# One PSUM tile per bank, and a new start-up, in a fused attention and channel-mix kernel

## The chip, the cores and the metric

The kernel runs on one core of one Trainium2 chip. The metric is the device time of one execution in microseconds (us). All runs that are compared below are in the fast state, with a granted TensorE clock of 0.96 to 1.00 of full; one run that was not is named where it occurs.

A ratio below is the mean time of one kernel's fast runs over the mean of the fast runs of the kernel before from the same rounds, with a 95% interval. It is therefore not quite the ratio of the medians that stand beside it.

Engine names: PE is TensorE, PEld its weight loads, DVE is VectorE, ACT is ScalarE, POOL is GpSimd, SP is SyncE.

## The reference

```python
# q, k, v: (8 batches, 8 heads, 576, 64) float32
q_s = softmax(q, axis=-1)
k_s = softmax(k, axis=2)                       # over the sequence
kv  = einsum('bhsd,bhse->bhde', k_s, v)
x   = einsum('bhsd,bhde->bhse', q_s, kv)       # then reshaped to (8, 576, 512)
x_prev = x shifted by one row, zero first
xk = mu_k * x + (1 - mu_k) * x_prev
xr = mu_r * x + (1 - mu_r) * x_prev
k   = maximum(xk @ w_k, 0)                     # 512 -> 1024
out = sigmoid(xr @ w_r) * (k * k @ w_v)        # 1024 -> 512
```

## The kernel before

The kernel loads q, k and v per batch in two groups of four heads, does the attention with small matmuls, and mixes rows into xk and xr. The rows then go through the second part in units of 512 (or 256) rows: K matmuls (`xk @ w_k`), relu on ACT, a square on DVE, R matmuls (`xr @ w_r`), tanh on ACT (the sigmoid), V matmuls (`k*k @ w_v`), and a gate on DVE that reads the V result from PSUM. A small planner written in the kernel orders every operation of every engine before it emits them. A framework below it sets the semaphores (counters by which one engine waits for another) from the tiles that each instruction touches.

The results of K, R and V lie in PSUM, the memory that takes the matmuls' results, in four banks that are used in turn. Before, these four banks are two tiles of two banks each; in batch 0 the kv matmuls borrow the same banks as a pair:

```python
banks = [psum.tile([128, 2, 512], F32, name=f"bank_{x}") for x in "abcd"]
ps = {"mm": [banks[2 + i // 2][:, i % 2, :] for i in range(4)],      # K, R, V
      "att": [t[:, :, :] for t in banks[0:2]],
      "early": [t[:, :, :] for t in banks[2:4]]}                     # kv of batch 0
# ... cut ...
def k_part(kf, fc, cts):                       # K: four matmuls of 512 columns
    for ct in cts:
        nc.tensor.matmul(bank(kf)[:, 0:n], lhsT=wk_bf[:, ct, fc * 128:(fc + 1) * 128],
                         rhs=xs[0][:, ct, c0:c0 + n], start=(ct == 0), stop=(ct == CT - 1))
# ... cut ...
nc.scalar.activation(out=rels[rel.index][:, 0:n], in_=bank(kf)[:, 0:n], func=ACT.Relu, ...)
# ... cut ...
nc.vector.scalar_tensor_tensor(out=ots[ot.index][:], in0=ths[th.index][:], scalar=1.0,
                               in1=bank(vps), op0=ALU.add, op1=ALU.mult)
```

The start-up: batch 0 comes in twelve pieces of 288 KB on the queues of SP and ACT, and the weights come on POOL's queue behind a wait on one of those pieces.

```python
gate = [first[GATE]]                           # GATE = 7: the second piece of v, group 0
# ... cut ...
if h == u == 0:
    tc.add_manual_dep(ld.ins, gate[0].made.ins.name, sync)
# in the planner: every operation's key is drawn forward by when its users are due, loads too
if closed:
    for o in after.get(op, ()):
        op.key = min(op.key, o.key - op.lat - HOP - SPARE)
```

The softmax here doesn't subtract the row's maximum and nothing guards it: scores larger than these inputs give would overflow.

## Time and profile before

| | before |
|---|---|
| time, median of 3 runs | 230.28 us (230.2 to 231.39) |
| span of the profiled run | 228.7 us |
| PE busy | 196.1 us, 86% |
| TensorE work, columns at 512 per 0.216 us (worked out) | 181.8 us |
| stalls between matmuls (worked out) | 33.7 us |

The page of the profile gives the busy time of each engine and, in 40 slices of 5.7 us, its busy share in tenths. These are its first lines for the kernel before:

```profile
span 228.7 us, 3591 instructions
...
PE 196.1 (86%) x1281; PEld 98.1 (43%) x1281; DVE 164.9 (72%) x368; ACT 152.3 (67%) x228; POOL 41.6 (18%) x65
...
PE   0076999967899878998979999999999999999881
...
DVE  1774855898899959989787989699578538832521
ACT  2658689798898688587427897957775664452430
...
```

PE is the busiest engine by far, and yet many slices stand at 7 or 8. A 9 stands for 90% or more, so it does not tell whether PE is full in the later slices, where DVE and ACT are half idle; the windows do.

The view of windows sums the busy time in stretches. Its columns are the stretch and, for each engine, busy us with the number of instructions, then the granted clock, the share of the DMA engines and GB/s:

```profile
...
core 0: us, PE busy (x) PEld busy (x) DVE busy (x) ACT busy (x) POOL busy (x), PEclk, DMA share, GB/s
34.00:54.00 20.00, 17.85 (x154) 9.16 (x152) 16.13 (x35) 18.46 (x27) 10.41 (x15) 1.00 1.04 400
54.00:94.00 40.00, 35.17 (x221) 17.02 (x221) 34.87 (x71) 33.86 (x47) 10.11 (x14) 1.00 0.90 317
94.00:214.00 120.00, 115.75 (x728) 56.82 (x727) 89.65 (x193) 74.92 (x114) 3.61 (x5) 1.00 0.32 80
...
```

From 94 us on ACT is busy 75 of 120 us and DVE 90, and PE still loses time. From 34 to 54 us ACT is nearly full.

The view of waits of the kernel before, from 54 us on and for PE, says whom each matmul waited for (total us, times, longest):

```profile
...
engine line waited for: us in total, times, longest us
PE bank_c L617 <- ACT rel_a L602: 1.6, 2, 1.3
PE bank_d L617 <- DVE ot_c L664: 1.2, 1, 1.2
PE bank_c L658 <- ACT th_b L653: 1.2, 2, 1.0
PE bank_c L658 <- DVE ot_b L664: 1.1, 2, 0.8
...
PE bank_c L648 <- ACT rel_c L602: 0.6, 1, 0.6
...
```

The matmuls wait for many different readers of PSUM: relu (`rel`) and tanh (`th`) on ACT, the gate (`ot`) on DVE. This list alone does not say whether the reader used the bank that the matmul wanted. Two readings do. The first is the built program: each semaphore wait names the instruction that must have finished, and 146 of its waits have as their only common ground a PSUM tile of which the two instructions touch different banks. The second is the chain of work that ended last. These are its pieces around 212 us (start, length, what):

```profile
...
210.17 1.74 PE bank_d L658 x8
...
211.99 0.70 DVE ot_c L664
...
212.73 1.04 PE bank_d L658 x4
...
```

Two V matmul groups are in flight here, one in each bank of tile `bank_d`. The first ends, the gate `ot_c` reads its bank, and only then do the last four V matmuls start, though they write the other bank. They wait for nothing else.

The start-up, from the timeline of the kernel before (start, length, engine, line, operation, and in brackets the idle time before it with what ended it):

```profile
...
4.66 2.51 POOL L351 DMA_DIRECT2D wk_bf<-in_moe_w_k_dram  x4
...
17.22 0.67 ACT L406 CAST vv_b<-raw_f 128x576 bf16<-128x576 f32 x1 [1.18 <-DMA raw_f<-in_v_dram]
...
19.38 0.67 ACT L406 CAST vv_b<-raw_f 128x576 bf16<-128x576 f32 x1
...
21.54 1.16 PE L429 MATMUL bank_d<-vv_b,ek_b 64*128 64x129 bf16 x18
...
22.63 1.44 PE L617 MATMUL bank_c<-xk,wk_bf 128*128 128x512 bf16 x4
...
26.49 1.02 PE L617 MATMUL bank_d<-xk,wk_bf 128*128 128x512 bf16 x4
...
34.98 1.03 PE L658 MATMUL bank_c<-wv_bf,k_a 128*128 128x512 bf16 x4
...
```

The weights are issued at 4.66 us, in the middle of batch 0's loads. v of group 1 is cast at 17.22 and 19.38 us when its pieces land, its kv matmuls run at 21.54 us, K runs steadily from 26.49 us, and V starts at 34.98 us.

### The profile page before, as it was taken

How to read it: one execution, taken by the hardware profiler on the slowest of the kernel's cores; microseconds unless marked ns; L12 is line 12 of the kernel's file. 1: busy time of each engine (PE TensorE's matmuls, PEld its weight loads, DVE VectorE, ACT ScalarE, POOL GpSimd, SP SyncE). 2: the span in 40 equal slices, each digit the busy share in tenths (PEclk: the TensorE clock that was granted, in tenths of full speed). 3: DMA queues.
4: the chain of work that ended last, by engine and by line, in shares of the span. 5: the costliest groups of instructions: out<-in, count | busy, mean ns of one | idle time of the engine just before them, and what ended most of it. 6: DMA issues, size and time to landing. Idle time of an engine off the chain costs nothing. (4 is left out here: it accounts for less than half of the span.)

```text
span 228.7 us, 3591 instructions
## 1 busy us (share of the span) xinstructions
PE 196.1 (86%) x1281; PEld 98.1 (43%) x1281; DVE 164.9 (72%) x368; ACT 152.3 (67%) x228; POOL 41.6 (18%) x65
## 2 busy tenths in 40 slices
PE   0076999967899878998979999999999999999881
PEld 0053444533354434543446544444543454444530
DVE  1774855898899959989787989699578538832521
ACT  2658689798898688587427897957775664452430
POOL 8615437344322122112000000000000000000000
PEclk9999999999999999999999999999999999999999
DMA  6999999999999858868372040222042122403404
GB/s 199 299 292 357 209 338 390 402 399 402 393 400 404 290 193 232 237 159 268 109 195 46 4 92 0 64 63 62 0 94 67 25 49 46 92 0 91 94 3 92
DMA packets 16722, 40.88 MB, mean 179 GB/s; under 512 B 2360, under 2 KB 5184, under 8 KB 16704
## 3 DMA queue, kind: packets, MB, share of 16 engines
q0 software_dynamic: 8896, 27.40, 37.3%
q1 hardware_dynamic: 7200, 12.39, 20.1%
q10 hardware_dynamic: 608, 0.85, 1.2%
q8 instruction: 10, 0.16, 0.3%
q14 instruction: 8, 0.07, 0.1%
HBM read 33.82 MB, written 9.44 MB: 189 GB/s over the span
## 5 line engine op out<-in xcount | busy, mean ns | idle before, releaser
L617 PEld LDWEIGHTS <-wk_bf 128*128 128x128 bf16 x320 | 30.6, 98 | 39.0 <-issue 9.9
L617 PE MATMUL bank_d<-xk,wk_bf 128*128 128x512 bf16 (+1 forms) x160 | 37.1, 357 | 3.5 <-DVE ot_c L664 1.2
L617 PE MATMUL bank_c<-xk,wk_bf 128*128 128x512 bf16 (+1 forms) x160 | 37.6, 360 | 2.3 <-ACT rel_a L602 1.6
L658 PEld LDWEIGHTS <-k_a 128*128 128x128 bf16 x144 | 13.5, 97 | 18.9 <-issue 3.0
L658 PE MATMUL bank_c<-wv_bf,k_a 128*128 128x512 bf16 x80 | 20.2, 379 | 1.3 <-ACT th_b L653 1.0
L658 PEld LDWEIGHTS <-k_b 128*128 128x128 bf16 x144 | 13.5, 97 | 17.5 <-issue 3.1
L648 PEld LDWEIGHTS <-xr 128*128 128x128 bf16 x144 | 13.3, 98 | 17.3 <-issue 2.4
L658 PE MATMUL bank_d<-wv_bf,k_b 128*128 128x512 bf16 x80 | 20.2, 379 | 0.3 <-DVE ot_b L664 0.3
L648 PE MATMUL bank_c<-wr_bf,xr 128*128 128x512 bf16 x72 | 18.5, 379 | 0.8 <-ACT rel_c L602 0.6
L648 PE MATMUL bank_d<-wr_bf,xr 128*128 128x512 bf16 x72 | 18.5, 379 | 0.5 <-ACT th_b L653 0.5
L658 PE MATMUL bank_d<-wv_bf,k_a 128*128 128x512 bf16 x64 | 16.1, 379 | 1.6 <-DVE ot_c L664 0.9
L658 PE MATMUL bank_c<-wv_bf,k_b 128*128 128x512 bf16 x64 | 16.2, 379 | 1.2 <-DVE ot_b L664 0.8
L602 ACT ACTIVATE rel_c<-bank_d 128x512 bf16<-128x512 f32 (+1 forms) x17 | 9.3, 547 | 8.7 <-PE bank_d L617 8.1
L602 ACT ACTIVATE rel_b<-bank_c 128x512 bf16<-128x512 f32 (+1 forms) x17 | 9.5, 559 | 5.9 <-PE bank_c L617 5.2
L653 ACT ACTIVATE th_a<-bank_c 128x512 f32<-128x512 f32 x10 | 6.0, 598 | 7.3 <-PE bank_c L648 3.4
L602 ACT ACTIVATE rel_a<-bank_c 128x512 bf16<-128x512 f32 (+1 forms) x14 | 7.5, 539 | 4.0 <-PE bank_c L617 3.8
L653 ACT ACTIVATE th_a<-bank_d 128x512 f32<-128x512 f32 x8 | 4.8, 599 | 6.4 <-PE bank_d L648 5.7
L602 ACT ACTIVATE rel_a<-bank_d 128x512 bf16<-128x512 f32 (+1 forms) x13 | 7.4, 570 | 1.8 <-PE bank_d L617 1.6
L606 DVE TENSOR_TENSOR k_a<-rel_b 128x512 bf16<-128x512 bf16 (+1 forms) x14 | 5.6, 404 | 3.9 <-ACT rel_b L602 3.7
L443 PE MATMUL bank_a<-ident,qs_a 128*128 128x128 bf16 x72 | 5.8, 230 | 2.8 <-DVE qs_a L421 2.8
L447 ACT COPY qt_a<-bank_a 128x1152 bf16<-128x1152 bf16 x5 | 5.6, 1117 | 3.7 <-PE bank_a L443 3.7
L653 ACT ACTIVATE th_b<-bank_c 128x512 f32<-128x512 f32 x8 | 4.8, 598 | 4.8 <-PE bank_c L648 4.5
(208 smaller groups left out, 389.0 us busy)
## 6 DMA issues: line engine op xcount, KB each, us to landing
out_dram<-ot_a SPq DMA_DIRECT2D x24, 128.0 KB, 2.4
out_dram<-ot_b SPq DMA_DIRECT2D x24, 128.0 KB, 2.4
out_dram<-ot_c SPq DMA_DIRECT2D x24, 128.0 KB, 2.4
raw_a<-in_q_dram POOLq DMA_DIRECT2D x3, 576.0 KB, 8.7
raw_b<-in_q_dram POOLq DMA_DIRECT2D x3, 576.0 KB, 7.0
raw_c<-in_k_dram POOLq DMA_DIRECT2D x3, 576.0 KB, 7.7
raw_d<-in_v_dram POOLq DMA_DIRECT2D x3, 576.0 KB, 8.5
raw_e<-in_k_dram POOLq DMA_DIRECT2D x3, 576.0 KB, 9.7
```

The source lines that it names most:

```text
L443: nc.tensor.transpose(out=transposed()[:, j, :], in_=qss[qs.index][:, j, :], identity=ident[:])
L447: nc.scalar.copy(out=qts[qt.index][:], in_=transposed()[:, 0:J, :])
L602: nc.scalar.activation(out=rels[rel.index][:, 0:n], in_=bank(kf)[:, 0:n], func=ACT.Relu, scale=HALF_ROOT)
L606: nc.vector.tensor_tensor(out=k2s[k2.index][:, fc, 0:n], in0=rels[rel.index][:, 0:n], in1=rels[rel.index][:, 0:n], op=ALU.mult)
L617: nc.tensor.matmul(bank(kf)[:, 0:n], lhsT=wk_bf[:, ct, fc * 128:(fc + 1) * 128], rhs=xs[0][:, ct, c0:c0 + n], start=(ct == 0), stop=(ct == ...
L648: nc.tensor.matmul(bank(rps), lhsT=xs[1][:, ct, c:c + 128], rhs=wr_bf[:, ct, :], start=(ct == 0), stop=(ct == CT - 1))
L653: nc.scalar.activation(out=ths[th.index][:], in_=bank(rps), func=ACT.Tanh, scale=0.5)
L658: nc.tensor.matmul(bank(vps), lhsT=k2s[k2.index][:, ft, 128 * m:128 * m + 128], rhs=wv_bf[:, ft, :], start=(ft == 0), stop=(ft == FT - 1))
```

## The change

Its intent: each matmul bank becomes its own tile, so that only accesses to one bank order each other; batch 0's pieces come in a fixed order with batch 0 ahead of the weights; the mask work of mu leaves DVE and ACT's queue for POOL.

```diff
-MU_KEY = (0.5, 1.9, LATE, LATE)
+FILL = 0
# planner
-                if closed:
+                if closed and not op.size:          # loads keep their own key
# PSUM
-    banks = [psum.tile([128, 2, 512], F32, name=f"bank_{x}") for x in "abcd"]
-    ps = {"mm": [banks[2 + i // 2][:, i % 2, :] for i in range(4)],
-          "att": [t[:, :, :] for t in banks[0:2]], "early": [t[:, :, :] for t in banks[2:4]]}
+    ps = {"mm": [psum.tile([128, 512], F32, name=f"mm_{x}") for x in "abcd"],
+          "att": [psum.tile([128, 2, 512], F32, name=f"att_{x}") for x in "ab"]}
+    def kv_of(slot, hf):                            # kv of batch 0: two tiles now
+        if slot.pool == "early":
+            return ps["mm"][2 * slot.index + hf][:]
+        return bank(slot)[:, hf, :]
# masks
-        nc.gpsimd.memset(mu_mask[:]..., 0.0)
+        nc.vector.memset(mu_mask[:]..., 0.0)
-            nc.scalar.dma_start(out=mu_rows[...], in_=ap)
+            nc.gpsimd.dma_start(out=mu_rows[...], in_=ap)
-            nc.vector.tensor_copy(out=mu_mask[...], in_=mu_rows[...])
-            nc.vector.tensor_scalar(out=mu_mask[...], in0=mu_rows[...], ...)
+            nc.gpsimd.tensor_copy(out=mu_mask[...], in_=mu_rows[...])
+            nc.gpsimd.tensor_scalar(out=mu_mask[...], in0=mu_rows[...], ...)
# cut: two reciprocals where kv lies in two tiles, planned durations, an unused filler (FILL = 0)
```

The wait that holds the weights is the same text as before (`GATE = 7`). What changes is when its piece comes: before, the planner drew that half of v to the head of SP's queue; with fixed order it is the eighth piece. That the planner does this is seen in the order of the built programs, not in the diff.

More of the change, by code (lines that the diff above doesn't have):

```diff
@@ L233 @@
     ots = buffers("ot", [128, C], F32)
-    banks = [psum.tile([128, 2, 512], F32, name=f"bank_{x}") for x in "abcd"]
-    ps = {"mm": [banks[2 + i // 2][:, i % 2, :] for i in range(4)],
-          "att": [t[:, :, :] for t in banks[0:2]], "early": [t[:, :, :] for t in banks[2:4]]}
+    ps = {"mm": [psum.tile([128, 512], F32, name=f"mm_{x}") for x in "abcd"],
+          "att": [psum.tile([128, 2, 512], F32, name=f"att_{x}") for x in "ab"]}
     def bank(slot):
-        return ps[slot.pool][slot.index]
+        return ps[slot.pool][slot.index][:]
+    def kv_of(slot, hf):
+        if slot.pool == "early":
+            return ps["mm"][2 * slot.index + hf][:]
+        return bank(slot)[:, hf, :]
     xs = [const.tile([128, CT, RING], BF16, name=n) for n in ("xk", "xr")]
@@ L300, in emit_mask_zeros @@
     def emit_mask_zeros():
-        nc.gpsimd.memset(mu_mask[:].rearrange("p m s c e -> p (m s c e)"), 0.0)
+        nc.vector.memset(mu_mask[:].rearrange("p m s c e -> p (m s c e)"), 0.0)
     def emit_late_consts():
@@ L310 @@
     plan.add("ACT", 2.0, 2.0, 1.5, emit_warm, [zero])
-    mu_load = plan.add("POOL", 1.2, 1.2, -9, emit_mu_load, size=8.0)
-    identity = plan.add("POOL", 0.6, 0.8, -8, emit_identity)
-    consts = plan.add("DVE", 0.5, 0.6, -9, emit_consts, [identity])
+    mu_load = plan.add("POOL", 1.2, 1.2, -9.2, emit_mu_load, size=8.0)
+    identity = plan.add("POOL", 0.6, 0.8, -9.1, emit_identity)
+    consts = plan.add("DVE", 0.2, 0.3, -9, emit_consts, [identity])
     late_consts = plan.add("DVE", 0.6, 0.7, LATE, emit_late_consts)
-    mask_zeros = plan.add("POOL", 2.2, 2.3, -7, emit_mask_zeros)
+    mask_zeros = plan.add("DVE", 1.8, 1.9, 0, emit_mask_zeros)
     mu_slot = Slot("mm")
@@ L328, in emit_mu_rows_load @@
             ap = bass.AP(tensor=src.tensor, offset=src.offset + 256 * u, ap=[[0, 64], [1, 256]])
-            nc.scalar.dma_start(
+            nc.gpsimd.dma_start(
                 out=mu_rows[64 * u:64 * u + 64, m, :, :].rearrange("p c e -> p (c e)"), in_=ap)
@@ L335, in emit_mu_mask, with filler @@
             r = slice(64 * u, 64 * u + 64)
-            nc.vector.tensor_copy(out=mu_mask[r, m, 0, :, r], in_=mu_rows[r, m, :, :])
-            nc.vector.tensor_scalar(out=mu_mask[r, m, 1, :, r], in0=mu_rows[r, m, :, :],
+            nc.gpsimd.tensor_copy(out=mu_mask[r, m, 0, :, r], in_=mu_rows[r, m, :, :])
+            nc.gpsimd.tensor_scalar(out=mu_mask[r, m, 1, :, r], in0=mu_rows[r, m, :, :],
                                     scalar1=-1.0, scalar2=1.0, op0=ALU.mult, op1=ALU.add)
     mu_t = plan.add("PE", 0.2, 0.4, -500, emit_mu, [mu_load, consts], [mu_slot])
-    mu_done = plan.add("DVE", 0.08, 0.17, LATE, emit_mu_copy, [mu_t], gives=[mu_slot])
+    mu_done = plan.add("DVE", 0.08, 0.17, 0, emit_mu_copy, [mu_t], gives=[mu_slot])
     mu_masked = []
     for m in range(2):
-        o = plan.add("ACT", 0.9, 0.9, MU_KEY[m], lambda m=m: emit_mu_rows_load(m), size=131.0)
-        mu_masked.append(plan.add("DVE", 1.0, 1.1, MU_KEY[2 + m], lambda m=m: emit_mu_mask(m),
+        o = plan.add("POOL", 1.4, 1.4, -9.5 + m, lambda m=m: emit_mu_rows_load(m), size=131.0)
+        mu_masked.append(plan.add("POOL", 1.6, 1.7, -2 + m, lambda m=m: emit_mu_mask(m),
                                   [o, mask_zeros]))
+    def filler(slot):
+        for _ in range(2):
+            nc.tensor.matmul(bank(slot)[:, 0:128], lhsT=ident[:], rhs=ident[:], start=True,
+                             stop=True)
+    for _ in range(FILL):
+        slot = Slot("mm")
+        plan.add("PE", 0.11, 0.2, 2 * LATE, lambda slot=slot: filler(slot), [identity], [slot],
+                 [slot])
     def weight_part(dst, src, n, u, c0, c1):
@@ L429, in kv @@
                     nc.tensor.matmul(
-                        bank(kvp)[:, hf, 0:129],
+                        kv_of(kvp, hf)[:, 0:129],
                         lhsT=eks[ek.index][r, j, :, :].rearrange("p u d -> p (u d)"),
@@ L434, in recz @@
         def recz():
-            nc.vector.reciprocal(out=rzs[rz.index][:, :, None],
-                                 in_=bank(kvp)[:, :, 128:129])
+            if kvp.pool == "att":
+                nc.vector.reciprocal(out=rzs[rz.index][:, :, None],
+                                     in_=bank(kvp)[:, :, 128:129])
+            else:
+                for hf in range(2):
+                    nc.vector.reciprocal(out=rzs[rz.index][:, hf:hf + 1],
+                                         in_=kv_of(kvp, hf)[:, 128:129])
         def transposed():
@@ L480, in attention @@
         kvm = plan.add("PE", 0.63, 0.7, pe_key, kv, expk + castv, [kvp], [ek, vv])
-        zdone = plan.add("DVE", 0.066, 0.15, step + 2, recz, [kvm], [rz])
+        zdone = plan.add("DVE", 0.08 * (2 if b == 0 else 1), 0.25 if b == 0 else 0.16, step + 2, recz, [kvm], [rz])
         def weights_of(wp, m, hf, s):
             nc.vector.scalar_tensor_tensor(
-                out=wps[wp.index][:, hf, s, :], in0=bank(kvp)[:, hf, 0:128],
+                out=wps[wp.index][:, hf, s, :], in0=kv_of(kvp, hf)[:, 0:128],
                 scalar=rzs[rz.index][:, hf:hf + 1], in1=mu_mask[:, m, s, 2 * g + hf, :],
@@ L571, in attention @@
                                 [xb] if hf == 0 else [], [xps[hf]]))
-        o = plan.add("DVE", 0.1, 0.19, step + 6, edge, evs)
+        o = plan.add("DVE", 0.11, 0.19, step + 6, edge, evs)
         xdiff = plan.add("DVE", 0.66, 0.755, step + 6, diff, [o], [xd])
```

## The prediction

> **What bounds it now.** TensorE. The page shows PE busy 196.1 of 228.7 us at full granted clock. Counting each matmul at the back-to-back pace of the trace (512 columns per 0.216 us), the program holds 179.4 us of TensorE work (my sum). The rest is about 19 us without work before the first K matmul at 22.6 us (timeline), 23 us of stalls between matmuls afterwards, and a tail of some 4 us. Windows view: from 34 to 54 us ACT is busy 18.5 of 20 us; from 94 to 134 us ACT and DVE have slack (25.9 and 33.7 of 40), yet PE still loses time.
>
> **Main term: PSUM tiles.** Before, one tile holds two banks, and the built program orders accesses by tile: 146 semaphore waits have as their only reason an access to the other bank of the same tile; in the changed program I count none. The Trainium skill, "PSUM — Partial Sum Buffer", "The four PSUM rules", says "Each bank is a separate physical SRAM", so these waits protect nothing; no run has shown that yet. Laid beside the trace, such waits hold back PE's start by 13.8 us in all after 22.6 us: 6.1 at K matmuls (L617), 5.6 at V (L658), 2.1 at R (L648). In the chain, the last V half waits from 222.2 to 223.0 us for a gate on DVE (ot_b) that reads the other bank. 4.3 us lie before 94 us, where ACT or data would often be the next wait (I count half, 2 us), 9.5 us after, where little else stalls PE (85%, 8 us).
>
> **Start-up.** Before, v's second half of group 0 is loaded first (SyncE, 0.74 us), so the weights' gate opens near 4.6 us and wk competes with batch 0; v of group 1 is cast only at 17.2 and 19.4 us, and K matmuls run steadily only from 26.5 us. After, the 12 batch-0 pieces go q, q, k, v, k, v and wk waits for the eighth, near 9 to 10 us. At the pace seen (0.85 us per 288 KB piece) all land by 13 to 14 us; kv of group 1 moves from 21.5 to about 16 us, steady K to about 20. But the weights come no sooner: DMA is nine tenths busy to 75 us, wv landed near 32.8 us before, and V cannot start much before 33. What survives is ACT and DVE work done ahead of the ACT-bound stretch: 2.5 us.
>
> **Small terms.** The mask arithmetic (8 instructions, 2.4 us) leaves DVE, the 1.8 us memset goes to it while idle: little. On GpSimd it is off the chain unless mask r is late. Later loads in fixed order: slots gate them, neutral.
>
> **Sum.** 230.3 - 8 - 2 - 2.5 gives about 217.5 us, 8 in 10 between 212.5 and 223. Chances: faster by over 2% 0.94, within 2% 0.05, slower 0.01.
>
> **What would show it.** Right: PE stalls from 94 us on fall from about 11 us to 2 to 4; PE waits on DVE ot and ACT rel/th nearly vanish from the waits view; wk issue moves from 4.7 to 9 or 10 us; kv of group 1 at 15 to 17 us; first V at 32 to 34 us. Wrong: stalls just move to true waits (same bank's reader), or first V comes after 35 us.
>
> **What would make it wrong.** Late weights stalling the first unit; ACT saturation giving back early gains; mm slots held long by mask r.

## The result and the profile after

| | before | after |
|---|---|---|
| time, median | 230.83 us (230.2 to 231.46, 4 runs) | 213.62 us (213.51 to 214.27, 4 runs) |
| ratio of fast runs | | 0.926 (0.9222 to 0.9299) |
| span of the profiled run | 228.7 us | 211.9 us |
| PE busy | 86% | 90% |

The same lines of the page, for the kernel after:

```profile
span 211.9 us, 3596 instructions
...
PE 190.7 (90%) x1281; PEld 97.1 (46%) x1281; DVE 163.0 (77%) x363; ACT 152.0 (72%) x228; POOL 45.1 (21%) x76
...
PE   0269788978999999999999999999999999999990
...
DVE  4958651999999999999988999698679448942521
ACT  3694796999899999697449987946794665452430
...
```

From the eleventh slice on PE stays at 9, up to the last one.

The windows of the kernel after; the last stretch ends where its matmuls near their end:

```profile
...
54.00:94.00 40.00, 39.92 (x299) 20.09 (x297) 39.29 (x84) 36.31 (x50) 12.24 (x18) 1.00 1.00 375
94.00:197.00 103.00, 103.00 (x659) 51.47 (x657) 80.87 (x175) 69.10 (x106) 2.12 (x3) 1.00 0.30 77
...
```

From 94 us on PE is busy 103.00 of 103 us, against 115.75 of 120 before. In the stretch from 54 to 94 us it is busy 39.92 of 40 us, up from 35.17, with DVE at 39.29 and ACT at 36.31: these two now do more in the same time as well.

The waits of PE over the whole span of the kernel after, part of its eight lines:

```profile
...
PE mm_c L443 <- ACT vv_a L420: 2.0, 1, 2.0
PE mm_c L636 <- DVE xk L579: 2.0, 1, 2.0
PE mm_d L677 <- DMA wv_bf<-in_moe_w_v_dram: 1.3, 1, 1.3
PE mm_c L636 <- ACT rel_a L621: 1.1, 1, 1.1
...
PE mm_c L636 <- ACT rel_c L621: 0.3, 1, 0.3
```

All of these lie before 54 us; the same view from 54 us on has no line at all. Of the reads that PE waited for before, those of DVE's gate and of tanh are gone.

The start-up of the kernel after, from its timeline:

```profile
...
7.86 0.94 POOL L340 COPY mu_mask<-mu_rows 64x256 f32<-64x256 f32 x1 [2.91 <-DMA mu_rows<-in_moe_mu_k_dram]
...
11.64 2.54 POOL L365 DMA_DIRECT2D wk_bf<-in_moe_w_k_dram  x4 [1.62 <-DMA raw_d<-in_v_dram]
...
14.12 1.23 ACT L420 CAST vv_b<-raw_f 128x576 bf16<-128x576 f32 x2
...
19.25 0.60 PE L636 MATMUL mm_c<-xk,wk_bf 128*128 128x512 bf16 x2
...
```

And its first V matmuls, from a later part of the same timeline:

```profile
...
32.36 1.02 PE L677 MATMUL mm_d<-wv_bf,k_a 128*128 128x512 bf16 x4 [1.28 <-DMA wv_bf<-in_moe_w_v_dram]
...
```

The weights are issued at 11.64 us, behind the masks on POOL and the eighth piece. v of group 1 is cast at 14.12 us, its kv matmuls follow at 15.40 us (before 21.54), steady K starts at 19.25 us (before 26.49). But V starts at 32.36 us, only 2.6 us sooner than before, and it waited for wv to land.

A sum that I worked out for several kernels from the start times of the matmuls: the stall before a matmul is the time from the start of the one before it, less that one's columns at 512 per 0.216 us, the pace at which matmuls follow each other in these traces (columns count half for the matmuls that use half of the rows and run in pairs). The prediction names this pace too, but its 179.4 us of work comes from one about 1% faster; at 0.216 us the kernels hold 181.8 us. "Other bank" is the part of it that a wait for the other bank of the same tile brought about, beyond what the true waits would have cost at that place. A second count by a slightly different rule gives 154 waits and 14.5 us for the kernel before, in place of 146 and 13.8, and none for after; the figures are good to about that much. Up to 22 of the 1281 matmul records are missing in the traces of some experiments; their work is counted from the program. The columns "tiles only", "paired tiles" and "early weights" are experiments of the next section.

```
stalls of PE, us            before   tiles only   paired tiles   after   early weights
0 to 54 us                   15.4       15.0          15.1        13.2       11.7
54 to 94 us                   7.0        0.9           4.1         1.6        1.4
94 us to the end             11.3        1.7           9.3         1.6        1.7
all                          33.7       17.6          28.5        16.4       14.7
of it "other bank"           13.8        0             9.3         0          0
```

### The profile page after: what moved, and what is told of

Same layout as the page of the kernel before. It is cut to its first block, busy times and chain, and to the rows that moved or that the text cites. A ratio compares the mean times of both kernels' runs of the same rounds, so it can differ in the third digit from the quotient of the medians.

```text
span 211.9 us, 3596 instructions
## 1 busy us (share of the span) xinstructions
PE 190.7 (90%) x1281; PEld 97.1 (46%) x1281; DVE 163.0 (77%) x363; ACT 152.0 (72%) x228; POOL 45.1 (21%) x76
## 4 chain that ended last, share of the span: by engine, by line
PE 70%; DMA 15%; DVE 6%; ACT 3%; SPq 1%; issue 1%; POOL 1%; DVEq 0%; POOLq 0%
PE mm_b L677 8%; PE mm_a L677 7%; PE mm_a L636 6%; PE mm_c L636 6%; PE mm_b L636 6%; PE mm_d L677 6%; PE mm_c L677 5%; PE mm_d L636 5%; PE mm_d L667 5%; DMA raw_l<-in_v_dram 4%; DMA wr_bf<-in_moe_w_r_dram 4%; DMA raw_d<-in_v_dram 4%; DMA wk_bf<-in_moe_w_k_dram 3%; PE mm_c L667 3%; PE mm_a L667 3%; PE att_b L443 2%
## 5 line engine op out<-in xcount | busy, mean ns | idle before, releaser
L636 PE MATMUL mm_c<-xk,wk_bf 128*128 128x512 bf16 (+1 forms) x88 | 21.7, 359 | 3.4 <-DVE xk L579 2.0
L677 PEld LDWEIGHTS <-k_a 128*128 128x128 bf16 x144 | 13.3, 98 | 16.3 <-issue 1.6
L636 PE MATMUL mm_a<-xk,wk_bf 128*128 128x512 bf16 (+1 forms) x84 | 20.5, 359 | 0.1
L667 PEld LDWEIGHTS <-xr 128*128 128x128 bf16 x144 | 13.3, 98 | 15.3
L636 PE MATMUL mm_d<-xk,wk_bf 128*128 128x512 bf16 (+1 forms) x72 | 18.0, 361 | 0.0
L636 PE MATMUL mm_b<-xk,wk_bf 128*128 128x512 bf16 (+1 forms) x76 | 17.7, 351 | 0.0
L677 PE MATMUL mm_b<-wv_bf,k_a 128*128 128x512 bf16 x56 | 14.4, 379 | 0.0
L667 PE MATMUL mm_d<-wr_bf,xr 128*128 128x512 bf16 x48 | 12.3, 380 | 0.0
L677 PE MATMUL mm_a<-wv_bf,k_b 128*128 128x512 bf16 x48 | 12.3, 379 | 0.0
L677 PE MATMUL mm_d<-wv_bf,k_a 128*128 128x512 bf16 x40 | 10.3, 379 | 1.3 <-DMA wv_bf<-in_moe_w_v_dram 1.3
L667 PE MATMUL mm_c<-wr_bf,xr 128*128 128x512 bf16 x40 | 10.3, 379 | 0.0
L677 PE MATMUL mm_b<-wv_bf,k_b 128*128 128x512 bf16 x40 | 10.1, 379 | 0.0
```

What stands on the lines that cost most here:

```text
L667: nc.tensor.matmul(bank(rps), lhsT=xs[1][:, ct, c:c + 128], rhs=wr_bf[:, ct, :], start=(ct == 0), stop=(ct == CT - 1))
L677: nc.tensor.matmul(bank(vps), lhsT=k2s[k2.index][:, ft, 128 * m:128 * m + 128], rhs=wv_bf[:, ft, :], start=(ft == 0), stop=(ft == FT - 1))
```

## Experiments

Twelve runs, of eleven kernels, were made in three calls. The kernel before ran beside each.

### The tiles alone

The kernel before with the new tiles and nothing else. The order of the instructions on each engine is the same as before, but for one more reciprocal in each of the two groups of batch 0.

```diff
-    banks = [psum.tile([128, 2, 512], F32, ...) for x in "abcd"]
-    ps = {"mm": [banks[2 + i // 2][:, i % 2, :] for i in range(4)], ...}
+    ps = {"mm": [psum.tile([128, 512], F32, name=f"mm_{x}") for x in "abcd"], "att": ...}
```

> The kernel before with one PSUM tile per bank and nothing else (every engine's instructions and their order stay, but for two more reciprocals of batch 0). If the cross-bank waits themselves cost the time, the stalls of TensorE after the first K matmul fall from 23 us to about 10 us and the time is 217 to 219.5 us (ratio about 0.945). If they hide behind true waits or the gain comes from the new start-up and plan, it stays at 225 us or more.

Measured: 215.07 us beside 230.05 us, ratio 0.9353 (0.9306 to 0.94). The tiles alone bring 15.0 us, more than expected. Windows and waits of PE from 54 us on:

```profile
...
54.00:94.00 40.00, 39.79 (x266) 20.03 (x269) 39.11 (x84) 36.19 (x50) 11.98 (x17) 1.00 0.98 360
94.00:198.00 104.00, 103.16 (x652) 51.91 (x662) 82.00 (x177) 69.93 (x107) 2.17 (x3) 1.00 0.32 78
...
```

```profile
...
PE mm_c L657 <- issue: 0.2, 1, 0.2
PE mm_b L657 <- issue: 0.2, 1, 0.2
```

PE is busy 39.79 of 40 us from 54 to 94 us, and it waits for no other engine from 54 us on. The span fell by 16.2 us (228.7 to 212.5), and the stalls by 16.1 us (33.7 to 17.6). So the gain is stalls, and nothing else. It is also more than the 13.8 us that stood at waits for the other bank: between 54 and 94 us the stalls that I had put down to true waits fell too, from 4.0 us (7.0 less 3.0) to 0.9. The program before also had 29 such waits of ACT on PE and 9 of DVE on PE; that these held back the true producers is the likely reason, but no run separates it.

### The rest alone

The kernel after with two banks per tile again, every instruction in the same order.

```diff
-    ps = {"mm": [psum.tile([128, 512], F32, name=f"mm_{x}") for x in "abcd"], ...}
+    mmt = [psum.tile([128, 2, 512], F32, name=f"bank_{x}") for x in "cd"]
+    ps = {"mm": [mmt[i // 2][:, i % 2, :] for i in range(4)], ...}
```

> The kernel after with two banks per PSUM tile again, every instruction and order kept. If the waits cost the time and the rest of the change is worth about 3 us: 226 to 228.5 us. If start-up and plan carry most of the gain: 219 us or less.

Measured: 224.99 us, ratio 0.9775 (0.9721 to 0.983). By the 2% rule this is unclear, but it is faster than before. It lies between the two expectations, so neither was right: the rest is worth more than the 3 us expected as long as tiles are paired. Against the 213.6 us of after the tiles are worth 11.4 us here. The rest is worth 5.1 us with paired tiles (230.05 to 224.99), and 1 to 2 us on top of split tiles (215.07 to 213.62 by the medians, which come from two calls; by the ratios, 0.9353 less 0.926, 2.1 us, and less the 0.9305 of after once more, 1.1 us). The two parts overlap, so their gains do not add.

### All four banks in one tile

```diff
+    mmt = psum.tile([128, 4, 512], F32, name="bank_q")
+    ps = {"mm": [mmt[:, i, :] for i in range(4)], ...}
```

> The kernel after with all four matmul banks in one PSUM tile, order kept: the suspected cost doubled (252 cross-bank waits in the program against 145 with two banks a tile). If the waits cost the time, clearly slower than with two banks a tile, by 6 us or more. If two banks a tile already cost all that can be lost, about the same as that kernel.

Measured: 325.29 us, ratio 1.4146 (1.4066 to 1.4227). The order of every engine is that of after; only what counts as one tile is different. The loss is far more than the 6 us expected. The page and the waits (ACT waits for matmuls of other banks, PE waits for ACT in turn):

```profile
span 324.2 us, 3590 instructions
...
PE 217.0 (67%) x1260; PEld 100.2 (31%) x1281; DVE 167.3 (52%) x363; ACT 155.1 (48%) x228; POOL 44.9 (14%) x76
...
```

```profile
...
ACT th_a L674 <- PE bank_q L679: 26.0, 12, 3.8
...
PE bank_q L638 <- ACT rel_a L623: 13.1, 19, 1.2
...
```

With one tile, the matmuls and the reads of their results nearly take turns: PE is busy 67%. The tanh reads the result of R (L669 in this kernel), and yet it waited 26.0 us for V matmuls (L679), which write another bank. This is the suspected cost made larger, and it answers as a cause should: 214, 225 and 325 us for 0, 145 and 252 such waits.

### The order of the loads

The kernel after with the planner's line as before, so that loads are drawn forward by their users.

```diff
-                if closed and not op.size:
+                if closed:
```

> The kernel after with loads ordered by when their users are due, as before, so that a half of v comes first and opens the weights' gate near 4.6 us. If the fixed order makes the start-up gain: 2 to 3 us slower than after, 216 to 217 us, first K matmul of the second unit back near 47 to 48 us from 44.9. If the order is neutral: 213 to 214.5 us.

Measured: 213.79 us, ratio 0.9289 (0.9241 to 0.9336): the order is neutral. The weights were issued at 5.4 us and wv landed at 30.2 and 32.7 us (32.3 and 34.9 in after), but batch 0's last piece landed at 16.7 us (14.3 in after). What the weights won, batch 0 lost: V started at 32.2 us, against 32.4. K of the second unit started at 44.0 us. This does not isolate the loads wholly, since the built program shows that the planner also ordered PE, ACT and DVE in another way here.

### The kernel after once more

> The kernel after once more, beside the runs of this call: 213 to 214.5 us, ratio to before 0.922 to 0.930.

Measured: 213.94 us, ratio 0.9305 (0.926 to 0.9351). This is the number to set beside the next three.

### The weights not held

Order and plan stay; the first weight waits on the first piece of batch 0 in place of the eighth.

```diff
-                tc.add_manual_dep(ld.ins, gate[0].made.ins.name, sync)
+                tc.add_manual_dep(ld.ins, first[0].made.ins.name, sync)
```

> The kernel after, every order kept, but the weights wait on the first piece of batch 0 (near 4.6 us) and no longer on the eighth (11.6 us). If what lands by about 33 and 39 us (wv, then v of batch 1) is set by the total of bytes, holding the weights is neutral for the end: kv of group 1 later by 2 us or more (17 to 19 us), the time within 0.7 us of after. If an early batch 0 is worth what it shows, 2 us slower than after.

Measured: 212.21 us, ratio 0.9209 (0.9164 to 0.9253), faster than after, which neither expectation had foreseen. One of its six runs, the profiled one, took 343.28 us at a granted clock of 0.576; it is not used in the ratio. So the run was repeated:

> The kernel with the weights held only by the first piece again, since its profile fell in a run at a granted clock of 0.576. If the release is really worth what the fast runs of the first time showed: 211.5 to 213 us, ratio to before 0.918 to 0.926, and the profile shows more TensorE work done by 54 us than the 31.7 us of after (some 32.5 to 33.5). If it was chance: 213.5 us or more. A second run at a low clock would tie that state to this kernel.

Measured: 212.01 us, ratio 0.9183 (0.9156 to 0.9209), four runs, all fast. It beats both kernels. By 54 us PE had done 33.7 us of work in the expectation's count (31.7 in after), just above the range expected. The issue of wk, from its timeline (start, length, what):

```profile
...
9.50 2.54 POOL L365 DMA_DIRECT2D wk_bf<-in_moe_w_k_dram  x4
...
```

And its first V matmuls, from a later part of the same timeline:

```profile
...
29.36 1.02 PE L677 MATMUL mm_d<-wv_bf,k_a 128*128 128x512 bf16 x4 [0.53 <-DMA wv_bf<-in_moe_w_v_dram]
...
```

The issue of wk moves only from 11.64 to 9.50 us, since it stands behind the masks in POOL's queue. In this profile batch 0 does not suffer: kv of group 1 runs at 15.3 us as in after. And everything behind wk on that queue moves by about 3 us: wv lands at 29.3 us in place of 32.3, v of batch 1 at 36.4 in place of 39.4, V starts at 29.36 us and K of the second unit at 41.9 us in place of 44.9. The profile of the first run of this kernel, taken again at a clock of 0.996, shows less: wk is issued at 9.51 us too, but wv lands at 29.9 us, V starts at 30.87 and K of the second unit at 43.4 us, and kv of group 1 runs only at 16.3 us. So V gains 1.5 to 3 us, and batch 0 can lose up to 1 us. By the times, holding the weights for the eighth piece costs about 2 us.

### The mask work back on DVE and ACT's queue

```diff
-        nc.vector.memset(mu_mask...)       ;  nc.gpsimd: mu_rows loads, mask copies
+        nc.gpsimd.memset(mu_mask...)       ;  nc.scalar: mu_rows loads;  nc.vector: mask copies
```

> The kernel after with mu's row loads on ACT's queue, the memset on GpSimd and the masks on VectorE, as before. If the mask move is small, as predicted: within 1 us of after. If it carries the start-up gain (freed DMA semaphores of the fast queues, 2.4 us off VectorE): 1.5 us or more slower, near the 215 us of the kernel before with split tiles.

Measured: 216.28 us, ratio 0.9399 (0.9355 to 0.9443): 2.3 us slower than after in the same call, so the prediction's "little" does not hold for the kernel that the planner makes of it. The planner made another order on PE, ACT and DVE here, so the 2.3 us is not one cause. In the kept profile 2.9 us of stalls lie after 94 us, where after has 1.6 and 1.7 us in its two profiles. So some 1.2 us are lost where no mask is used, and go with the other order. What the trace shows: the mu loads took the place of raw pieces on the fast queues (raw pieces of k and v of group 1 were issued at 7.7 to 9.5 us, in after at 5.0 to 6.9), and kv of group 1 ran at 17.0 us. R of the first unit ran at 34.3 us in place of 30.1, but that is the order: V stands before it here, and V started at 32.6 us, as late as in after.

### Fewer bytes: wv not loaded

The result is wrong on purpose: wv is filled by a memset on POOL.

```diff
-        nc.gpsimd.dma_start(out=wv_bf[:, h * n:(h + 1) * n, :], in_=ap)
+        nc.gpsimd.memset(wv_bf[:, h * n:(h + 1) * n, :]..., 0.03125)
```

> Wrong result on purpose: the kernel after, but wv is filled by a memset on GpSimd in the same place instead of being loaded (2.1 MB of reads less), order kept. If the DMA stream eats the start-up gain: the 1.3 us wait for wv at the first V matmul goes, v of batch 1 lands some 4 to 5 us sooner, K of the second unit starts at 41 to 43 us from 44.9, and the time falls by 2 to 4 us (210 to 211.5). If ACT's load between 24 and 54 us is what holds it: K of the second unit stays at 44 to 45 us and the time within 1 us.

Measured: 212.78 us, ratio 0.9241 (0.9187 to 0.9296), 1.2 us under after in the same call, but the intervals overlap. It lies between the two expectations and is inconclusive as a test. Two profiles of it differ. In the first R waited 1.2 us for wr and started at 31.5 us, and V at 32.4 us. In the one kept, wr landed at 30.4 us (29.9 and 30.3 in the two profiles of after), R started at 30.8, V at 31.7 and K of the second unit at 44.2 us (44.9 and 45.5 in those of after). What it does show is that v of batch 1 was not what the second unit waited for: v landed 4.2 us sooner (35.2 us), and K of that unit still came 12.55 us behind the first V, as in after.

### Less load on ACT, less on DVE

Both results are wrong on purpose: the casts of v (ACT), or the row sums (DVE), of batch 1 work on 8 of 64 columns.

```diff
+            w = 8 if b == 1 else D
-            copy(out=to[:, :, u, :], in_=...)
+            copy(out=to[:, :, u, 0:w], in_=...[:, :, :, 0:w])          # ACT
-            nc.vector.reduce_sum(out=sums(rsums, u), in_=eqs[eq.index][:, :, u, :], axis=AX.X)
+            nc.vector.reduce_sum(out=sums(rsums, u), in_=eqs[eq.index][:, :, u, 0:w], axis=AX.X)
```

> Wrong result on purpose: the kernel after, with the four casts of v of batch 1 on ScalarE cut from 64 to 8 of each 64 columns (about 1.5 us off ScalarE between 26 and 40 us), orders kept. If ScalarE's load is what eats the start-up gain: K of the second unit 1 us or more sooner than 44.9 us and 1 to 1.5 us off the time (212 to 212.8). If VectorE or data hold it: within 0.5 us of 213.8.

> Wrong result on purpose: the kernel after, with the four row sums of batch 1 on VectorE taken over 8 of 64 columns (about 1.8 us off VectorE between 22 and 39 us), orders kept. If VectorE's chain holds the second unit: 1 us or more off the time. If ScalarE or data hold it: within 0.5 us of 213.8.

Measured: 213.80 us (ratio 0.9262, 0.9241 to 0.9284) and 214.09 us (0.9293, 0.923 to 0.9355). Neither moves the time. So cutting 1.5 us off ACT or 1.8 us off DVE between 22 and 40 us gains nothing, although ACT is busy 18.6 of 20 us from 34 to 54 us. First V stood at 32.4 and 33.0 us. In after, early weights, the wv test and these two the second unit's K came 12.5 or 12.6 us behind the first V, wherever that was. The matmuls in between hold 11.9 us of work, so PE is nearly full there, and it is the first V that counts. One stall is left behind it in all of these: K waits 1.7 to 2.0 us for xk, near 48 us in after, and no run took it away.

### A try at more: v casts of batch 1 on POOL

```diff
+            if b == 1:
+                castv.append(plan.add("POOL", ..., lambda u=u: cast_v(nc.gpsimd.tensor_copy, u), ...))
```

> A try at a faster version: weights held only by the first piece, and the casts of v of batch 1 on GpSimd, which takes 2.4 us off ScalarE. If ScalarE holds the first 54 us: 1 us or more under the version with the early gate alone. If GpSimd's casts get in the way of its DMA issues or of VectorE: no gain or slower.

Measured: 217.66 us, ratio 0.9429 (0.9409 to 0.945): 5.6 us slower than early weights alone. The planner's order differs here on PE, ACT and DVE as well. From its timeline:

```profile
...
41.82 0.71 POOL L271 DMA_DIRECT2D raw_j<-in_q_dram  x1 [1.20 <-ACT qt_a L466]
...
43.44 0.71 POOL L271 DMA_DIRECT2D raw_k<-in_k_dram  x1 [0.91 <-ACT ek_a L413]
44.14 1.28 POOL L420 CAST vv_b<-raw_l 128x576 bf16<-128x576 f32 x2
45.48 1.16 PE L443 MATMUL att_b<-vv_b,ek_b 64*128 64x129 bf16 x18 [4.87 <-POOL vv_b L420]
...
```

v of group 1 had landed at 37.9 us. Its cast stood on POOL behind eleven DMA issues, several of which wait, as in the first two lines, for ACT, and ran at 44.14 us; PE idled 4.87 us for it.

## Why the prediction was right

The time of 213.62 us lies in the range of 212.5 to 223, near its lower end, and the main mechanism was right. Point by point:

- **Main term.** "I count half, 2 us" and "85%, 8 us" are the mis-sized terms. I had 10 us for the tiles; alone they bring 15.0 us. Discounting a wait because "ACT or data would often be the next wait" was the error: all 13.8 us went, and some 3 us of stalls at true waits with them. Stalls from 94 us on fell from 11.3 to 1.6 us; I had said 2 to 4.
- **Start-up.** The moves came as predicted (kv of group 1 at 15.4 us, steady K at 19.3, V at 32.4), and the sense that little survives was right: 1 to 2 us on top of the tiles, against 2.5. "The weights come no sooner" was too mild: the first half of wv landed 3 us later than before (32.3 against 29.1 us), since the gate shifts everything behind it on POOL's queue. The limit of 33 us for V seems to have been read from the landing of wv's second half (32.2 us before), while the first V needs only the first half. That V came at 32.4 us as forecast is owed to the later gate, so this figure was partly luck; with early weights V came at 29.4 and 30.9 us. wk was issued at 11.6 us and not at 9 to 10.
- **What survives.** I gave ACT's full stretch as the limit. Taking 1.5 us off ACT, or 1.8 us off DVE, ahead of and at the start of that stretch changed nothing; shifting the weights did.
- **Small terms.** "Little" was too low for the masks: undoing that move cost 2.3 us, about half of it with the planner's other order. Undoing the fixed order of the loads changed nothing (213.79 us), as said for the later batches.
- **Sum.** Too little for the tiles and too much for the start-up partly cancel: 12.5 us predicted, 17.2 us measured.

On the page that the prediction cites: the Trainium skill, "PSUM — Partial Sum Buffer", "The four PSUM rules", calls each bank a separate physical SRAM. No run shows that they are separate memories, but the runs agree with what follows from it: with no waits between banks, the results stay correct and 15.0 us are gained. The same page's "Summary: rules for kernel authors" says to read a different bank while a matmul runs and to "sem-guard by bank", which is what the new tiles make the framework do.

## What to carry to other kernels

Declare PSUM (and any buffer used in turn) in tiles as small as the unit that is handed over, then count in the built program the waits whose two sides touch different banks; here their stalls needed no discount for the next true wait (13.8 us read, 15.0 us gained), likely because the readers were held back as well. Follow a gain at the start to the next thing that lands late: here batch 0 came 6 us sooner, and the first V matmul, which waits for weights on an in-order queue, decided what was kept. Be wary of compute on a queue whose DMA issues have to wait: the one try here lost 5.6 us.

## What the Trainium skill lacked or had wrong

- "PSUM — Partial Sum Buffer" tells to guard by bank, but no page says that a layer which places the semaphores may guard by tile: two banks per tile made 146 needless waits and 15.0 us, four banks per tile 252 waits and 325 us in place of 214.
- "DMA: Bandwidth & Descriptors", "Issuing engines are not separate DMA queues", says that issuing from several engines "will only save the time on the sequencer". It does not say what an issue that is held by a wait does to those behind it on its queue. Here that counted: wk at 9.50 in place of 11.64 us moved the later landings by 2 to 3 us and the time by about 2 us.
- "GPSIMD Engine Reference", "Elementwise — side-by-side cycle accounting", gives GpSimd as 1.96 times slower for a two-input add. For the one-input copy of 64x256 fp32 the traces show a median of 0.394 us on GpSimd (after) and 0.292 us on VectorE (before), four copies each, a ratio of 1.35; the table has no entry for a copy.
- "TensorE: Matmul & The Clock Gate" tells of a lower clock while TensorE idles and when a third core of a die starts dense matmuls. One of ten executions of the kernel with early weights, on one core, took 343.28 us at a granted clock of 0.576, and the next stood at 0.996 again. No run here shows which of the two it was, or whether it was either.
